# Exponentials shared by three engines: the whole powers made on GpSimd, the gate sums on TensorE, both query masks in one step

## The chip, the cores and the metric

The kernel runs on one core of a Trainium2 chip. The core has five engines with a queue each, which run side by side and wait for each other by semaphores: TensorE (PE; its weight loads are shown as PEld), VectorE (DVE), ScalarE (ACT), GpSimd (POOL) and SyncE (SP), whose queue issues most DMA transfers. Each engine takes its instructions in the order in which they stand. The metric is the device time of one execution in microseconds; lower is better.

## The reference

One input `x` of 2048 rows of 512 goes through an attention block A and a mixer block B; a gate of each row mixes the two.

```python
def _A_ref(x, wqkv, wo):                      # H = 32 heads of Dh = 16
    qkv = (lambda x, *d: x.transpose(*d))((x @ wqkv).reshape(B, S, 3, H, Dh), 2, 0, 3, 1, 4)
    scores = jnp.einsum("bhqd,bhkd->bhqk", q, k) * (Dh ** -0.5)
    p = _softmax(scores, axis=-1)
    o = jnp.einsum("bhqk,bhkd->bhqd", p, v)
    return (lambda x, *d: x.transpose(*d))(o, 0, 2, 1, 3).reshape(B, S, D) @ wo
...
    h = _gelu(_layernorm(x, axis=-1) @ w1)    # B: then four groups of columns shifted by rows, @ w2
    x1 = x + hs
    h2 = _gelu(_layernorm(x1, axis=-1) @ w3) @ w4
    return x1 + h2
...
g = _sigmoid((x * gate_w).sum(-1, keepdims=True))
return g * a + (1 - g) * b
```

All inputs are 16-bit floats (bfloat16). With 32 heads, 2048 queries and 2048 keys there are 134 million exponentials.

## The kernel before, in words

**Attention.** Work goes by units `(c, u)`: a chunk `c` of 512 queries and four heads `u`, 32 units. For each of 16 key tiles `kt` (128 keys) and each head `j` of the unit there is a block of scores, 128 keys by 512 queries, made by one matmul (`score`, L634). Two or three blocks share a stage of PSUM, and one ScalarE instruction takes the exponential of the stage (`expo`, L723) into `pt`; a matmul per block then multiplies `pt` with the values and adds into `acc` (`attend_block`, L731). The 1868 blocks that go this way make 694 exponentials: 34 early ones over two blocks, then two or three blocks each. The code calls each of the 694 a slot.

**The blocks that ScalarE does not do.** In each unit but the first two, 6 of 64 blocks (180 in all) get their exponential from VectorE and GpSimd instead. Their scores go to a PSUM tile `dsc` beside a stage of two blocks. `whole` (L638) then does for one block:

- L652, VectorE: `y`, a 32-bit integer, the score in units of 2^-16 of a power of two. Its upper 16 bits are the whole power, its lower 16 the fraction.
- L657 and L659, GpSimd: from the lower halves (every second 16-bit word of `y`), the two factors `ec` and `ea` of a polynomial, 16-bit floats.

Two blocks make a pair, and when the second is there VectorE does four steps of 1024 elements, each due a slot after the one before, the first three slots after the second block: `square` (L663), `one` (L667), `cubic` (L671, which leaves a bfloat16 between 1 and 2, times a constant) and `power` (L679). `power` takes the upper halves of `y`, times 128, and adds them to the bits of `ec` as 16-bit integers, by a scalar_tensor_tensor; this puts the whole power into the exponent. The pair then goes to TensorE like a `pt` (L731, `acc<-ec,vp`). `y` has two buffers, each of a pair and held from L652 to L679; `ea` has two, `ec` three.

**What sets the order.** The order of each engine's instructions is written out by the kernel: a loop over slots (L884 onward) emits the exponential of slot i, the scores of slot i+2, the matmuls with the values, a portion of other TensorE work (`beside`: projections, the mixer block, output tiles), a filling of idle matmuls with zeros (`fill`, L874), and then the VectorE steps that are due (`run_due`, L558). `due(slots, rank, cost, fn)` puts a step off by some slots. `run_due` sorts what is due by rank, and lets a step wait, by at most four slots, while the kernel's own reckoning of the engines' clocks says that VectorE is too far behind TensorE (`HORIZON`). A step in `asides` is taken one at a slot when there is time. `hurry` forces steps when a third pair or a second chain is open.

Scores of slot k+2 use the banks of slot k. They wait for the exponential of slot k, and where `dsc` was in use, for L652.

**Gate.** For each of 16 row tiles, `gate(t)` (L361) is an aside: VectorE multiplies `x` by the gate weights, spread over all partitions (`gw_b`, L137), and sums them into `g_raw` (L363, with a read of the accumulator). When the last is done, ScalarE takes a tanh (L367), VectorE makes `g_fin` (L369). The asides of the first LayerNorm's statistics (L277) stand between them.

**Query projections.** `q_proj` (L241) makes the queries of two units at once and leaves them in `qT` twice, each time with the other unit's 16 rows of 32 set to zero: two tensor_scalar steps by a mask column (L247).

Of the kernel before, what the change touches and what calls it, by code (L numbers as in the profile page):

```python
# [30 lines left out]
def kernel(  # L31
# [20 lines left out]
    KT = D // P  # L52
    NT = S // P
# [27 lines left out]
    ypool = ctx.enter_context(tc.tile_pool(name="ypool", bufs=2))  # L81
# [12 lines left out]
    gw_b = const.tile([P, D], BF16, name="gw_b")  # L94
# [42 lines left out]
    nc.sync.dma_start(out=gw_b[:], in_=gate_w.partition_broadcast(P))  # L137
# [29 lines left out]
    HORIZON = 1.9  # L167
    OVER = 4
# [72 lines left out]
    def q_proj(c, G):  # L241
        ps = gen("ps_q")
        qT = qpool.tile([P, 2, CH], BF16, tag="qT", name="qT")
        qTs[(c, G)] = qT
        yield from proj(ps, wq, slice(G * P, (G + 1) * P), xT[c])
        for a in range(2):
            evac(0.75).tensor_scalar(out=qT[:, a, :], in0=ps[:], scalar1=mask[:, a:a + 1], scalar2=None,  # L247
                                    op0=ALU.mult)
        made.add(("q", c, G))
        yield MM  # L250
        yield FREE
# [109 lines left out]
    def gate(t):  # L361
        scr = xnpool.tile([P, CH], BF16, tag="xn", name="scr")
        vec(0.77).tensor_tensor_reduce(  # L363
            out=scr[:], in0=x_sb[t][:], in1=gw_b[:], scale=1.0, scalar=0.0,
            op0=ALU.mult, op1=ALU.add, accum_out=g_raw[:, t:t + 1])
        if t == NT - 1:
            due(3, FIRST, 0.0, lambda: nc.scalar.activation(  # L367
                out=g_t[:], in_=g_raw[:], func=ACT.Tanh, scale=0.5))
            due(5, FIRST, 0.2, lambda: nc.vector.tensor_scalar(  # L369
                out=g_fin[:], in0=g_t[:], scalar1=0.5, scalar2=0.5, op0=ALU.mult, op1=ALU.add))  # L370

    def first_asides():
        for t in range(NT):
            asides.append(lambda t=t: ln_stats(0, t))
            asides.append(lambda t=t: gate(t))
        norm(0, 0)
# [109 lines left out]
    def early():  # L486
        for w in "v0 v1 k1 v2 v3 v4 k2 v5 v6 v7 v8 v9 k3 v10 v11 v12 v13 v14 v15".split():
            if w == "v1":
                first_asides()
            yield from (v_proj(int(w[1:])) if w[0] == "v" else k_proj(0, int(w[1:])))  # L490
        for G in range(1, NU // 2):
            for c in range(NC_):
                yield from k_proj(G, c)
            if G == 1:
                yield from q_proj(0, G)
        yield from mlp()
        state["done"] = True
# [60 lines left out]
    def run_due(all=False, only=(FIRST, CHAIN, LAST, TAIL)):  # L558

        now, state["force"] = state["slot"], all  # L560
        for item in sorted((x for x in later if x[0] <= now and x[1] in only), key=lambda x: (x[1], x[0], x[2])):
            _, _, _, cost, fn = item
            if cost and not all and max(clock["vector"], clock["act"]) + cost > clock["pe"] + HORIZON and now < item[0] + OVER:
                continue
            later.remove(item)
            fn()
        if TAIL in only and asides and now >= EARLY // 2 and max(clock["vector"], clock["act"]) + 0.7 < clock["pe"] + HORIZON:
            asides.popleft()()
# [69 lines left out]
    def whole(dsc, c, u, kt, j):  # L638


        if state["half"] == 0:
            while state["pairs"] == 3 or state["chains"] == 2:
                hurry()
            state["pairs"] += 1
            state["chains"] += 1
            halves["now"] = (ypool.tile([P, 2, CH], I32, tag="y", name="y"), epool.tile([P, 2, CH], F16, tag="ea", name="ea"),
                             ecpool.tile([P, 2, CH], F16, tag="ec", name="ec"), [])
        y, ea, ec, pair = halves["now"]
# [3 lines left out]
        vec(0.69, clock["pe"] + 0.2).tensor_scalar(out=y[:, r, :], in0=dsc[:], scalar1=65536.0 * DH ** -0.5 / LN2,  # L652
                                                   scalar2=-126.0 * 65536.0, op0=ALU.mult, op1=ALU.max)
        lo = y[:, r, :].bitcast(U16).rearrange("p (n k) -> p n k", k=2)[:, :, 0]
# [5 lines left out]
                                scalar2=root * CUB * IM * IM * (REAL - LN2 / 2), op0=ALU.mult, op1=ALU.add)  # L660

        def square():
            vec(0.75).tensor_tensor(out=ec[:], in0=ec[:], in1=ec[:], op=ALU.mult)  # L663
            due(1, CHAIN, 0.45, one)

        def one():
            vec(0.45).tensor_scalar(out=ec[:], in0=ec[:], scalar1=1.0, scalar2=None, op0=ALU.add)  # L667
            due(1, CHAIN, 0.7, cubic)

        def cubic():  # L670
            vec(0.75).tensor_tensor(out=ec[:].bitcast(BF16), in0=ec[:], in1=ea[:], op=ALU.mult)  # L671
            due(1, CHAIN, 1.23, power)

        def power():

            bits = ec[:].bitcast(I16)
            hi = y[:].bitcast(I16).rearrange("p r (n k) -> p r n k", k=2)[:, :, :, 1]
            state["chains"] -= 1
            vec(1.23).scalar_tensor_tensor(out=bits, in0=hi, scalar=128.0, in1=bits, op0=ALU.mult, op1=ALU.add)  # L679
            due(1, LAST, 0.0, lambda: products.append((c, u, pair, ec[:].bitcast(BF16))), "pe")  # L680

        if r == 1:
            due(3, CHAIN, 0.7, square)
# [239 lines left out]
```

## Time and profile before

| | |
|---|---|
| Runs shown | 927.56, 933.54, 933.91 us; median 933.54 |
| The profiled execution | 926.85 us, its span 925.1 us |
| Mean granted clock of TensorE | 0.982 |
| ScalarE busy | 884.4 us, 96% of the span |
| VectorE busy | 754.1 us, 82% |
| GpSimd busy | 313.0 us, 34% |
| L723, exponentials | 694, 854.6 us in all |
| L679, power | 90, 117.9 us in all, 1310 ns each |
| L657 and L659, GpSimd's two steps | 180 each, 811 and 828 ns each |
| L363, gate sums | 16, 702 ns each |
| L247, query masks | 30, 744 ns each |

How to read it: busy time is the union of an engine's instructions. A row of a group gives the line, the engine, the operation, output from inputs, shapes and number, then the busy time in us, the mean duration of one in ns, and after a second bar the time that the engine stood idle just before such instructions, with what ended it. Instructions of one engine overlap a little, so that the mean times the number can be more than the busy time: two exponentials over three blocks take 2.79 us together, one of them 1.45. The profile's matmul durations are modelled.

### The profile page before, as it was taken

What the parts mean: (1) busy time and instruction counts of PE and PEld (TensorE: products, weight loads), DVE (VectorE), ACT (ScalarE), POOL (GpSimd) and SP (SyncE); (2) the same over time, 40 slices, a digit from 0 to 9 for tenths busy, and PEclk for the clock granted to TensorE, in tenths of its full rate; (3) what the DMA queues carried; (4) which work ended last, traced back from release to release, by engine and by line L of the source; (5) the groups of instructions that cost most, each with busy time, mean ns of one, the idle gap of its engine ahead of it and who ended that gap; (6) DMA issues with size and microseconds to landing.
All of it is one profiled execution on the core that took longest, in us unless ns stands there. A gap on an engine that the chain in (4) does not pass through costs nothing.

```text
span 925.1 us, 14505 instructions
## 1 busy us (share of the span) xinstructions
PE 796.2 (86%) x5478; PEld 245.1 (26%) x5581; DVE 754.1 (82%) x1160; ACT 884.4 (96%) x735; POOL 313.0 (34%) x401
## 2 busy tenths in 40 slices
PE   7998888888888788899988889988889888889886
PEld 2222322222222222222222222222222222222221
DVE  3778888989899898877899967899976789876656
ACT  6889999999999999999999999999999999999993
POOL 3014334343444333433333333333244234333430
PEclk9998999999999999999999999999999999999998
DMA  9601000000000000000000000100000000000000
GB/s 218 198 13 58 1 13 13 13 14 2 13 12 13 13 13 5 10 13 24 25 13 2 12 13 13 36 13 13 1 12 13 13 13 8 29 13 13 13 13 23
DMA packets 30382, 22.28 MB, mean 24 GB/s; under 512 B 16744, under 2 KB 25832, under 8 KB 30312
## 3 DMA queue, kind: packets, MB, share of 16 engines
q1 hardware_dynamic: 28680, 20.17, 7.6%
q10 hardware_dynamic: 1632, 1.18, 0.5%
q8 instruction: 43, 0.70, 0.3%
q14 instruction: 27, 0.22, 0.1%
HBM read 17.17 MB, written 2.35 MB: 21 GB/s over the span
## 4 chain that ended last, share of the span: by engine, by line
ACT 45%; issue 19%; PE 16%; DVE 15%; DMA 4%; ACTq 0%; DVEq 0%; SPq 0%
ACT pt L723 43%; PE stage L634 5%; PE acc L731 3%; DVE ec L679 2%; DMA bcs<-rec_d 2%; DVE y L652 2%; ACT sq L345 2%; PE ps_k L222 1%; PE ps_v L222 1%; PE acc L874 1%; PE ps_o L222 1%; DMA rec_d<-rec 1%; PE ps L222 1%; DVE ec L671 1%; DVE yh L328 1%
## 5 line engine op out<-in xcount | busy, mean ns | idle before, releaser
L723 ACT ACTIVATE pt<-stage 128x1536 bf16<-128x1536 f32 (+1 forms) x694 | 854.6, 1413 | 20.6 <-PE stage L634 18.1
L634 PE MATMUL stage<-qT,kT 32*128 32x512 bf16 x1868 | 278.3, 387 | 100.9 <-ACT pt L723 73.8
L657 POOL TENSOR_SCALAR ec<-y 128x512 f16<-128x512 uint16 x180 | 145.9, 811 | 504.2 <-DVE y L652 504.0
L731 PE MATMUL acc<-pt,vp 128*17 128x512 bf16 (+1 forms) x1868 | 190.5, 389 | 1.0 <-DVE accsb L766 0.6
L634 PEld LDWEIGHTS <-kT 32*128 32x128 bf16 x2048 | 95.7, 91 | 344.7 <-issue 277.4
L652 DVE TENSOR_SCALAR y<-dsc 128x512 int32<-128x512 f32 x180 | 123.3, 685 | 52.5 <-PE dsc L634 51.0
L659 POOL TENSOR_SCALAR ea<-y 128x512 f16<-128x512 uint16 x180 | 149.1, 828 | 14.3
L874 PE MATMUL acc<-wq,zero 128*128 128x512 bf16 x396 | 137.5, 387 | 4.8 <-issue 4.8
L679 DVE SCALAR_TENSOR_TENSOR ec<-y,ec 128x1024 int16<-128x1024 int16 x90 | 117.9, 1310 | 1.1
L222 PE MATMUL ps_y<-xnT,w 128*128 128x512 bf16 x257 | 88.7, 393 | 3.3 <-DVE yh L328 1.6
L731 PEld LDWEIGHTS <-vp 128*17 128x17 bf16 (+1 forms) x2048 | 49.4, 88 | 121.6 <-issue 117.2
L671 DVE TENSOR_TENSOR ec<-ec,ea 128x1024 bf16<-128x1024 f16 x90 | 67.5, 751 | 3.6
L634 PE MATMUL dsc<-qT,kT 32*128 32x512 bf16 x180 | 70.4, 391 | 0.0
L222 PE MATMUL ps<-w,g2T 128*128 128x512 bf16 x208 | 63.1, 383 | 2.0 <-issue 1.9
L663 DVE TENSOR_TENSOR ec<-ec 128x1024 f16<-128x1024 f16 x90 | 63.2, 703 | 1.5 <-POOL ec L657 1.5
L328 DVE TENSOR_SCALAR yh<-ps_y 128x512 bf16<-128x512 f32 x72 | 49.4, 686 | 18.3 <-PE ps_y L222 16.2
L667 DVE TENSOR_SCALAR ec<-ec 128x1024 f16<-128x1024 f16 x90 | 45.9, 510 | 0.9
L874 PEld LDWEIGHTS <-zero 128*128 128x128 bf16 x430 | 32.9, 98 | 48.8 <-issue 48.6
L345 ACT ACTIVATE sq<-sq 128x1024 bf16<-128x1024 bf16 x36 | 41.6, 1155 | 1.5 <-DVE sq L340 1.5
L349 DVE SCALAR_TENSOR_TENSOR g2T<-sq,yh 128x1024 bf16<-128x1024 bf16 x28 | 38.5, 1379 | 0.0
L731 PE MATMUL acc<-ec,vp 128*17 128x512 bf16 x180 | 35.7, 390 | 2.4 <-DVE ec L679 2.4
L785 DVE TENSOR_TENSOR oT<-accsb,bcs 128x512 bf16<-128x512 f32 x31 | 22.4, 722 | 18.3 <-DMA bcs<-rec_d 18.2
(80 smaller groups left out, 510.7 us busy)
## 6 DMA issues: line engine op xcount, KB each, us to landing
bcs<-rec_d SPq DMA_DIRECT2D x31, 256.0 KB
w<-in_B_w_dram SPq DMA_DIRECT2D x2, 1792.0 KB
x_sb<-in_A_x_dram SPq DMA_DIRECT2D x14, 128.0 KB
out_dram<-ot SPq DMA_DIRECT2D x14, 128.0 KB
w<-in_B_w_dram SPq DMA_DIRECT2D x2, 512.0 KB
wkv<-in_A_wqkv_dram ACTq DMA_DIRECT2D x1, 512.0 KB
wo_pad<-in_A_wo_dram SPq DMA_DIRECT2D x8, 64.0 KB
den<-accsb SPq DMA_DIRECT2D x31, 8.0 KB
```

Of the source, the lines that this page charges most:

```text
L222: nc.tensor.matmul(*args, **kwargs)
L345: nc.scalar.activation(out=sq[:], in_=sq[:], func=ACT.Tanh)
L634: nc.tensor.matmul(out, lhsT=kT[G][32 * j:32 * j + 32, cc, o:o + P], rhs=qTs[(c, G)][32 * j:32 * j + 32, a, :], start=True, stop=True, til ...
L652: vec(0.69, clock["pe"] + 0.2).tensor_scalar(out=y[:, r, :], in0=dsc[:], scalar1=65536.0 * DH ** -0.5 / LN2, scalar2=-126.0 * 65536.0, op0 ...
L657: nc.gpsimd.tensor_scalar(out=ec[:, r, :], in0=lo, scalar1=g / IM, scalar2=(RE - LN2 / 2) / IM, op0=ALU.mult, op1=ALU.add)
L659: nc.gpsimd.tensor_scalar(out=ea[:, r, :], in0=lo, scalar1=root * CUB * IM * IM * g, scalar2=root * CUB * IM * IM * (REAL - LN2 / 2), op0= ...
L663: vec(0.75).tensor_tensor(out=ec[:], in0=ec[:], in1=ec[:], op=ALU.mult)
L671: vec(0.75).tensor_tensor(out=ec[:].bitcast(BF16), in0=ec[:], in1=ea[:], op=ALU.mult)
L679: vec(1.23).scalar_tensor_tensor(out=bits, in0=hi, scalar=128.0, in1=bits, op0=ALU.mult, op1=ALU.add)
L723: nc.scalar.activation(out=pt[:, 0:w], in_=stages.pop(k)[:, 0:w], func=ACT.Exp, scale=DH ** -0.5)
L731: nc.tensor.matmul(accs[(c, u)][32 * j:32 * j + M, :], lhsT=lhsT, rhs=p, start=(kt == 0), stop=(kt == NT - 1), skip_group_check=True, tile ...
L874: nc.tensor.matmul(acc[:], lhsT=zero[:], rhs=wq[:, 0, :], start=False, stop=False, skip_group_check=True)
```

## The change

- `whole` gets a third GpSimd step per block: the upper halves of `y` times 128, as 16-bit floats, into a new tile `nk` (two buffers of a pair). `y` is now a tile of one block, still with two buffers, read by GpSimd alone.
- `power` adds `nk` to the bits of `ec` by a plain tensor_tensor.
- `square` is due two slots after the second block (`CLAG`), not three. The other lags have a name and stay at one.
- The gate's 16 VectorE sums and their asides go. `gates()` runs on TensorE between the last key projection and the mixer block: for each row tile four matmuls of one column, with `x` transposed as the weights, into one PSUM tile; VectorE copies the 16 columns out. The gate weights are loaded as four columns of 128 (`gw`) and not spread over the partitions.
- `q_proj` writes both masked halves by one tensor_tensor, with the projection and the mask broadcast.
- `run_due` picks the next item anew after each step, in place of a list sorted once.

```diff
-    gw_b = const.tile([P, D], BF16, name="gw_b")
+    gw = const.tile([P, KT], BF16, name="gw")
...
-    nc.sync.dma_start(out=gw_b[:], in_=gate_w.partition_broadcast(P))
+    nc.sync.dma_start(out=gw[:], in_=gate_w.rearrange("(kt p) -> p kt", p=P))
...
+    CLAG = 2
+    NLAG = 1
...
-        for a in range(2):
-            evac(0.75).tensor_scalar(out=qT[:, a, :], in0=ps[:], scalar1=mask[:, a:a + 1], scalar2=None,
-                                    op0=ALU.mult)
+        evac(1.25).tensor_tensor(out=qT[:], in0=ps[:].unsqueeze(1).to_broadcast([P, 2, CH]),
+                                 in1=mask[:].unsqueeze(2).to_broadcast([P, 2, CH]), op=ALU.mult)
...
-    def gate(t):
-        scr = xnpool.tile([P, CH], BF16, tag="xn", name="scr")
-        vec(0.77).tensor_tensor_reduce(
-            out=scr[:], in0=x_sb[t][:], in1=gw_b[:], scale=1.0, scalar=0.0,
-            op0=ALU.mult, op1=ALU.add, accum_out=g_raw[:, t:t + 1])
...
+    def gates():
+
+        ps = gen("ps_g")
+        for t in range(NT):
+            c, o = divmod(t * P, CH)
+            clock["pe"] = max(clock["pe"], clock["bank"])
+            for kt in range(KT):
+                nc.tensor.matmul(ps[:, t:t + 1], lhsT=xT[c][:, kt, o:o + P], rhs=gw[:, kt:kt + 1],
+                                 start=(kt == 0), stop=(kt == KT - 1))
+            tensor("full", 0.3)
+            if t < NT - 1:
+                yield 0.3
+        evac(0.2).tensor_copy(out=g_raw[:], in_=ps[:, 0:NT])
+        due(3, FIRST, 0.0, lambda: nc.scalar.activation(out=g_t[:], in_=g_raw[:], func=ACT.Tanh, scale=0.5))
+        due(6, FIRST, 0.2, lambda: nc.vector.tensor_scalar(
+            out=g_fin[:], in0=g_t[:], scalar1=0.5, scalar2=0.5, op0=ALU.mult, op1=ALU.add))
...
-            asides.append(lambda t=t: gate(t))
...
+        yield from gates()
         yield from mlp()
...
-        for item in sorted((x for x in later if x[0] <= now and x[1] in only), key=lambda x: (x[1], x[0], x[2])):
+        passed = []
+        while True:
+            items = [x for x in later if x[0] <= now and x[1] in only and x not in passed]
+            if not items:
+                break
+            item = min(items, key=lambda x: (x[1], x[0], x[2]))
...
+                passed.append(item)
                 continue
...
+        y = ypool.tile([P, CH], I32, tag="y", name="y")
...
+        hi = y[:].bitcast(I16).rearrange("p (n k) -> p n k", k=2)[:, :, 1]
...
+        nc.gpsimd.tensor_scalar(out=nk[:, r, :], in0=hi, scalar1=128.0, scalar2=None, op0=ALU.mult)
...
-            due(1, CHAIN, 1.23, power)
+            due(NLAG, CHAIN, 0.75, power)
...
-            hi = y[:].bitcast(I16).rearrange("p r (n k) -> p r n k", k=2)[:, :, :, 1]
             state["chains"] -= 1
-            vec(1.23).scalar_tensor_tensor(out=bits, in0=hi, scalar=128.0, in1=bits, op0=ALU.mult, op1=ALU.add)
+            vec(0.75).tensor_tensor(out=bits, in0=bits, in1=nk[:], op=ALU.add)
...
-            due(3, CHAIN, 0.7, square)
+            due(CLAG, CHAIN, 0.7, square)
```

More of the change, by code (lines that the diff above doesn't have):

```diff
@@ L52 @@
     KT = D // P
+    YBUFS = 2
     NT = S // P
@@ L80 @@
     fin = ctx.enter_context(tc.tile_pool(name="fin", bufs=1))
-    ypool = ctx.enter_context(tc.tile_pool(name="ypool", bufs=2))
+    ypool = ctx.enter_context(tc.tile_pool(name="ypool", bufs=YBUFS))
+    nkpool = ctx.enter_context(tc.tile_pool(name="nkpool", bufs=2))
     epool = ctx.enter_context(tc.tile_pool(name="epool", bufs=2))
@@ L359 @@
     g_fin = const.tile([P, NT], F32, name="g_fin")
-    def gate(t):
-        scr = xnpool.tile([P, CH], BF16, tag="xn", name="scr")
-        vec(0.77).tensor_tensor_reduce(
-            out=scr[:], in0=x_sb[t][:], in1=gw_b[:], scale=1.0, scalar=0.0,
-            op0=ALU.mult, op1=ALU.add, accum_out=g_raw[:, t:t + 1])
[L366 to L370, printed above, removed]
+    def gates():
[13 more added lines that the diff above has]
+            out=g_fin[:], in0=g_t[:], scalar1=0.5, scalar2=0.5, op0=ALU.mult, op1=ALU.add))
+        yield 0.3
+        yield FREE
     def first_asides():
@@ L645, in whole @@
             state["chains"] += 1
-            halves["now"] = (ypool.tile([P, 2, CH], I32, tag="y", name="y"), epool.tile([P, 2, CH], F16, tag="ea", name="ea"),
+            halves["now"] = (nkpool.tile([P, 2, CH], F16, tag="nk", name="nk"), epool.tile([P, 2, CH], F16, tag="ea", name="ea"),
                              ecpool.tile([P, 2, CH], F16, tag="ec", name="ec"), [])
-        y, ea, ec, pair = halves["now"]
+        nk, ea, ec, pair = halves["now"]
+        y = ypool.tile([P, CH], I32, tag="y", name="y")
         r = state["half"]
@@ L651, in whole @@
         pair.append((kt, j))
-        vec(0.69, clock["pe"] + 0.2).tensor_scalar(out=y[:, r, :], in0=dsc[:], scalar1=65536.0 * DH ** -0.5 / LN2,
+        vec(0.69, clock["pe"] + 0.2).tensor_scalar(out=y[:], in0=dsc[:], scalar1=65536.0 * DH ** -0.5 / LN2,
                                                    scalar2=-126.0 * 65536.0, op0=ALU.mult, op1=ALU.max)
-        lo = y[:, r, :].bitcast(U16).rearrange("p (n k) -> p n k", k=2)[:, :, 0]
+        lo = y[:].bitcast(U16).rearrange("p (n k) -> p n k", k=2)[:, :, 0]
+        hi = y[:].bitcast(I16).rearrange("p (n k) -> p n k", k=2)[:, :, 1]
         g = LN2 / 65536.0
@@ L660, in whole @@
                                 scalar2=root * CUB * IM * IM * (REAL - LN2 / 2), op0=ALU.mult, op1=ALU.add)
+        nc.gpsimd.tensor_scalar(out=nk[:, r, :], in0=hi, scalar1=128.0, scalar2=None, op0=ALU.mult)
         def square():
             vec(0.75).tensor_tensor(out=ec[:], in0=ec[:], in1=ec[:], op=ALU.mult)
-            due(1, CHAIN, 0.45, one)
+            due(NLAG, CHAIN, 0.45, one)
         def one():
             vec(0.45).tensor_scalar(out=ec[:], in0=ec[:], scalar1=1.0, scalar2=None, op0=ALU.add)
-            due(1, CHAIN, 0.7, cubic)
+            due(NLAG, CHAIN, 0.7, cubic)
         def cubic():
             vec(0.75).tensor_tensor(out=ec[:].bitcast(BF16), in0=ec[:], in1=ea[:], op=ALU.mult)
-            due(1, CHAIN, 1.23, power)
+            due(NLAG, CHAIN, 0.75, power)
         def power():
             bits = ec[:].bitcast(I16)
-            hi = y[:].bitcast(I16).rearrange("p r (n k) -> p r n k", k=2)[:, :, :, 1]
             state["chains"] -= 1
-            vec(1.23).scalar_tensor_tensor(out=bits, in0=hi, scalar=128.0, in1=bits, op0=ALU.mult, op1=ALU.add)
+            vec(0.75).tensor_tensor(out=bits, in0=bits, in1=nk[:], op=ALU.add)
             due(1, LAST, 0.0, lambda: products.append((c, u, pair, ec[:].bitcast(BF16))), "pe")
         if r == 1:
-            due(3, CHAIN, 0.7, square)
+            due(CLAG, CHAIN, 0.7, square)
     def scores(k):
```

## The prediction

> **What bounds the kernel now.** I read the page first: the busy shares, then the costliest groups (busy us, mean ns of one, then the engine's idle time before them and what ended it).
>
> ```profile
> PE 796.2 (86%) x5478; PEld 245.1 (26%) x5581; DVE 754.1 (82%) x1160; ACT 884.4 (96%) x735; POOL 313.0 (34%) x401
> ...
> L723 ACT ACTIVATE pt<-stage 128x1536 bf16<-128x1536 f32 (+1 forms) x694 | 854.6, 1413 | 20.6 <-PE stage L634 18.1
> ...
> L657 POOL TENSOR_SCALAR ec<-y 128x512 f16<-128x512 uint16 x180 | 145.9, 811 | 504.2 <-DVE y L652 504.0
> ...
> L679 DVE SCALAR_TENSOR_TENSOR ec<-y,ec 128x1024 int16<-128x1024 int16 x90 | 117.9, 1310 | 1.1
> ...
> L671 DVE TENSOR_TENSOR ec<-ec,ea 128x1024 bf16<-128x1024 f16 x90 | 67.5, 751 | 3.6
> ...
> L663 DVE TENSOR_TENSOR ec<-ec 128x1024 f16<-128x1024 f16 x90 | 63.2, 703 | 1.5 <-POOL ec L657 1.5
> ```
>
> ScalarE's 694 exponentials (one per 854.6/694 = 1.23 us) fill the span; the change keeps all 694 and the 36 tanh, as the order of the built program shows. So only ScalarE's idle 925.1 − 884.4 = 40.7 us can move. The busy time by stretch says where that is:
>
> ```profile
> 0.00:60.00 60.00, 52.78 (x304) 16.20 (x310) 34.20 (x75) 43.80 (x44) 10.47 (x33) 0.97 0.63 162
> 60.00:100.00 40.00, 36.65 (x254) 10.97 (x255) 33.22 (x66) 37.87 (x32) 13.72 (x18) 0.91 0.13 38
> 100.00:900.00 800.00, 690.77 (x4838) 213.32 (x4927) 671.39 (x1001) 791.77 (x654) 288.77 (x351) 0.99 0.04 13
> 900.00:925.10 25.10, 15.96 (x92) 4.61 (x92) 15.30 (x20) 10.93 (x8) 0.00 (x0) 0.87 0.06 21
> ```
>
> (The fourth busy figure is ScalarE's.) It idles 16.2 us before 60 (loads, then TensorE's projections), 2.1 in 60 to 100, only 8.2 in 100 to 900, 14.2 at the end. The timeline names each gap of the 8.2; this is one of them:
>
> ```profile
> 801.92 1.22 DVE L679 SCALAR_TENSOR_TENSOR ec<-y,ec 128x1024 int16<-128x1024 int16 x1
> ...
> 803.66 0.69 DVE L652 TENSOR_SCALAR y<-dsc 128x512 int32<-128x512 f32 x1
> ...
> 804.41 0.39 PE L634 MATMUL stage<-qT,kT 32*128 32x512 bf16 x3 [1.11 <-DVE y L652]
> ...
> 804.90 1.45 ACT L723 ACTIVATE pt<-stage 128x1536 bf16<-128x1536 f32 x1 [0.85 <-PE stage L634]
> ```
>
> The power step (and the next pair's square, at 803.06) stand ahead of y on VectorE; the next scores wait 1.11 for y, which frees their bank; the exponential comes 0.85 late. Sorted by such causes: VectorE late (y, the power step, the GELU's sq), nine gaps, 0.32+0.16+0.59+0.56+0.24+0.54+0.93+0.20+0.85 = 4.4 us; TensorE at half the granted clock (stretches of 3.4 us from 151, 331, 465, 663, 741), 2.7; runs of five or more projections between two scores, 1.1. The waits put it in proportion:
>
> ```profile
> PEld L634 <- DVE y L652: 30.8, 51, 1.6
> ...
> PE stage L634 <- DVE y L652: 7.9, 15, 1.1
> ```
>
> TensorE's loads and matmuls wait 38.7 us for y in all, yet ScalarE's gaps of that kind are a ninth of it: the scores are made about one exponential ahead, so that lead has to be used up first. VectorE at 82% is thus not the bound, and an engine made lighter is worth here only what it takes out of the few late cases.
>
> **The change, part by part.**
>
> *Power step.* 90 × 1.310 leave VectorE. The two-operand add of 1024 16-bit elements has a near row on either side: 0.703 (L663, one tensor twice) and 0.751 (L671, two tensors); if it is not packed, 1.31 stays. I take L671's: 67.6 against 117.9, −50.3 us.
>
> *Whole powers on GpSimd.* 180 × 0.811 (L657; fastest 0.617, longest 1.862) = +146 us, 313 to 459, half the span. Its queue gets a third instruction per block. From the end of ea to the next ec's start it has 2.77 us in the median, 0.51 at the least, 1.22 at the twentieth, so nk fits nearly always. The add comes 3.6 us or more after ea's end by today's spacing, so it finds nk made: hidden, by less than a slot more if GpSimd is held up. A buffer of nk is written again two pairs later, some 18 us on, when its add is long past; y, now one block a buffer and read by GpSimd alone, is written again two blocks later, 9 us on. What stays uncovered is the square, moved from three slots behind y to two: today it starts 2.82 us after the second ec ends (median), 1.64 at the tenth, 1.07 at the twentieth, 0.03 at the least. Less 1.23, about one square in fifteen would wait, with y and the evacuations behind it on VectorE's queue and the scores behind y. I charge ScalarE +0.3 us; bounds 0 and 13 (rival D).
>
> *Contention.* VectorE's steps run longer where GpSimd runs beside more than 60% of them: L663 0.660 alone, 0.714 beside; L671 0.684 and 0.783; the tensor_scalar L667 0.416 and 0.615. The excess over undisturbed ones is some 31 us in all VectorE groups; with 459/313 of the GpSimd time, +14.
> The Trainium skill ("SBUF — State Buffer", section "Who interferes with whom") speaks against this change: such VectorE steps and a GpSimd step that reads SBUF exclude each other, and the second "fully blocks". By it each nk would cost its whole 0.617, +111 in place of +14. The trace agrees that they slow each other, but the lengthening seen (0.05 to 0.20 us) is far less than 0.617; starts put off are not ruled out.
>
> *Gate sums.* Sixteen VectorE sums leave, 11.2 + 1.3 = −12.5 us, one copy comes (+0.2). In their place come 64 one-column matmuls with 128x128 loads, in some eight slots after the key projections. Nearest row: four 128-column transposes with such loads take 0.40 us, 0.06 each after the first; above, 0.097, the load's own row. So 4 to 6 us of TensorE, up to 16 in one slot (1.0 to 1.6 us against 1.23 of lead): +0.4 us for ScalarE, bounds 0 and 1.2. The gate-weight load stays on SP's queue ahead of the wo, w3 and w4 loads, in smaller pieces; before's issue took 0.50 us at 20 us, and the gate matmuls come 60 us later: 0.
>
> *Masks.* A pair took 1.41 us in the timeline; one step of 1024 at full width is nearest to L679's 1.22 undisturbed (0.75 if packed, 1.4 disturbed): 15 × −0.2 = −2.9.
>
> VectorE: 754 − 50 − 12 − 3 + 14 = about 703. What ScalarE gets of it: in three gaps (0.59, 0.93, 0.85) a power step stands directly ahead and ends 0.56 sooner, −1.7; of the other 2.0 of that kind I take half, −1.0 (bounds together 0 and −4.4). What is late next there is GELU's last step, L349, 1.38 us long in places ahead of y, which the change leaves. In 60 to 100, 1.7 us of gaps follow a wait of 1.12 for y at 83 and a half-clock stretch from 82.3 to 89.1; half, −0.8 (bounds 0, −1.7). At 48.8 a 2.9 us wait for kT stays: LN statistics take the gates' place in the queue. The end: before, two fillers and two late ec products run between the last pt products and the copy of acc (912.5 to 913.4); in the new order they stand earlier, −0.65. The tail behind it is the same. The new loop in run_due picks the same items, since every follow-up is due a slot later at the earliest: 0.
>
> Sum: −1.7 − 1.0 − 0.8 − 0.65 + 0.4 + 0.3 = −3.45: 926.85 to 923.4. The profiled execution is 0.7% under the median, 933.54; the four executions shown (926.85, 927.56, 933.54, 933.91) lie in two groups, mean 930.5, for a cause that no view shows. I put the forecast beside that mean, +3.6: **927.0**.
>
> **Rivals.**
> - B, more: all late gaps, the half-clock ones and those at 82 to 90 go: 4.4 + 2.7 + 1.7 + 0.65 = 9.4, 917.5, with the +3.6: 921. For: some stretches of half clock follow starved matmuls. Against: others follow none that VectorE caused.
> - C, nothing: the add is not packed or the gaps just move; 930.5. For: ScalarE felt a tenth of VectorE's lateness.
> - E, the two engines shut each other out: each of 180 nk holds a VectorE step for the 0.617 of L657's shortest; VectorE 754 − 65 + 111 = 800, busier than before, and lateness of 4.4 + 1.7 half as long again, +3: 933.5. Against: the measured lengthening. This is the Trainium skill's rule, cited under contention.
> - D, slower: the square, now first in VectorE's queue a slot earlier, waits for GpSimd's ec. If it holds the queue 1.0 us on average, the y's behind pass the exponential's lead: today y starts more than 0.90 us after its scores in a quarter of cases; 180 / 4 × 0.3 = +13: 943.5. It decides from a mean wait of about 0.9 us. Against: 1.6 us of median slack left.
>
> **How the numbers follow.** A, the forecast: 0.56, own range 921 to 933. B 0.12, C 0.15, E 0.07, D 0.10. The range 919.5 to 936.5 leaves out D and the lower half of B. Over 1% (about what a measurement of this kernel can tell from no change) faster means under 924.2: B and a quarter of A, 0.26. Slower means over 942.9: D, 0.10. Within: 0.64.
>
> **What would show it.** The add's row at 0.70 to 0.80 with 90 of them; nk near 0.8; POOL about 459, DVE about 703; ACT idle in 100 to 900 down from 8.2 to about 5.5; a small wait of the square for ec. A square waiting often, or ScalarE's gaps unchanged at VectorE 703, would make it wrong.

## The result, and the profile after

The changed kernel takes 939.88 us (median of 20 runs) against 930.56 us for the kernel before on the same chip (20 runs): ratio 1.0089, 95% interval 1.0069 to 1.011. It is slower by 0.9%, where 927.0 us and a small gain were forecast. A run that stands far above the others of its kernel (here one of 1106.13 us, at a granted clock of 0.556) is left out of every ratio. The profiled execution took 940.16 us, its span 938.4, at a mean granted clock of 0.963 (before: 0.982). The two profiled executions lie 13.3 us apart and the medians 9.3, because the one of before (926.85 us) was among its quicker ones.

The page of the changed kernel: the busy shares, then the groups that answer to those shown of before (busy us, mean ns of one, then the engine's idle time before them and its causes).

```profile
PE 830.3 (88%) x5650; PEld 248.3 (26%) x5650; DVE 726.4 (77%) x1114; ACT 887.6 (95%) x735; POOL 606.3 (65%) x581
...
L742 ACT ACTIVATE pt<-stage 128x1536 bf16<-128x1536 f32 (+1 forms) x694 | 853.5, 1377 | 29.8 <-PE stage L651 24.3
...
L680 POOL TENSOR_SCALAR nk<-y 128x512 f16<-128x512 int16 x180 | 306.1, 1701 | 14.3
L676 POOL TENSOR_SCALAR ec<-y 128x512 f16<-128x512 uint16 x180 | 132.2, 735 | 235.5 <-DVE y L670 232.6
...
L698 DVE TENSOR_TENSOR ec<-ec,nk 128x1024 int16<-128x1024 int16 x90 | 77.4, 860 | 5.6
...
L683 DVE TENSOR_TENSOR ec<-ec 128x1024 f16<-128x1024 f16 x90 | 72.1, 801 | 8.3 <-POOL ec L676 7.7
L691 DVE TENSOR_TENSOR ec<-ec,ea 128x1024 bf16<-128x1024 f16 x90 | 72.2, 802 | 3.8
```

VectorE did get lighter, by 28 us (754.1 to 726.4). But nk takes 1701 ns, twice its price, the square and L691 each grew (703 to 801, 751 to 802), and the exponentials now wait 24.3 us for TensorE where they waited 18.1. (The trace of before has 5478 matmul records beside 5581 weight loads, the trace here 5650 of both. Some records of before are thus missing, so TensorE's busy times are not compared.)

Busy time by stretch, changed kernel; the fourth busy figure is ScalarE's, and the one behind GpSimd's is the granted clock.

```profile
0.00:60.00 60.00, 54.33 (x303) 16.53 (x303) 34.11 (x73) 42.78 (x43) 12.20 (x35) 0.94 0.62 160
60.00:100.00 40.00, 38.34 (x340) 13.07 (x337) 23.04 (x41) 39.84 (x34) 20.46 (x23) 1.00 0.15 39
100.00:900.00 800.00, 709.69 (x4845) 210.56 (x4843) 647.26 (x972) 779.84 (x641) 563.67 (x515) 0.97 0.04 13
900.00:938.40 38.40, 27.90 (x178) 8.10 (x176) 22.00 (x31) 25.13 (x20) 9.95 (x10) 0.91 0.06 21
```

ScalarE's idle time by these rows, against before: 17.2 (16.2), 0.2 (2.1), **20.2 (8.2)**, 13.3 (14.2). The span grew 13.3 us: 12.0 of it is idle time in 100 to 900 and 3.2 is more busy time, while the other stretches idle 1.8 us less. So the loss is spread through the middle of the kernel. The waits of the changed kernel over its whole span (us in total, times, longest):

```profile
DVE oT L804 <- DMA bcs<-rec_d: 24.7, 20, 3.1
...
PEld L651 <- DVE y L670: 23.8, 39, 1.9
...
DVE ec L683 <- POOL ec L676: 7.7, 10, 1.4
PE stage L651 <- DVE y L670: 5.8, 7, 1.6
```

TensorE waits less for y than before (29.6 against 38.7), the square waits for GpSimd (before: 1.5 us in 3 waits), and one wait has grown that the prediction did not name: VectorE's `oT`, which multiplies a finished attention tile by reciprocals that come back by DMA, from 18.2 us in 13 waits to 24.7 in 20. Its row before was:

```profile
DVE oT L785 <- DMA bcs<-rec_d: 18.2, 13, 2.7
```

The timeline shows one of these (start, duration, instruction, idle time before it and its cause):

```profile
265.14 2.39 ACT L742 ACTIVATE pt<-stage 128x1024 bf16<-128x1024 f32 x2
...
265.94 0.69 DVE L804 TENSOR_TENSOR oT<-accsb,bcs 128x512 bf16<-128x512 f32 x1 [1.72 <-DMA bcs<-rec_d]
...
266.55 0.69 DVE L280 BATCH_NORM_STATS2 st<-x_sb 128x6 f32<-128x512 bf16 x1
267.27 0.18 DVE L281 BATCH_NORM_AGGREGATE mv<-st 128x2 f32<-128x6 f32 x1
267.37 0.66 DVE L670 TENSOR_SCALAR y<-dsc 128x512 int32<-128x512 f32 x1
...
268.08 0.39 PE L651 MATMUL stage<-qT,kT 32*128 32x512 bf16 x3 [1.39 <-DVE y L670]
...
268.58 1.45 ACT L742 ACTIVATE pt<-stage 128x1536 bf16<-128x1536 f32 x1 [1.05 <-PE stage L651]
```

Read it downwards: VectorE stands 1.72 us at `oT`, with statistics and y behind it in its queue; y frees the bank 1.39 us late for TensorE's scores; the exponential is 1.05 us late.

### The profile page after: what moved, and what is told of

Same layout as the page of the kernel before. It is cut to its first block, busy times and chain, and to the rows that moved or that the text cites. A ratio compares the mean times of both kernels' runs of the same rounds, so it can differ in the third digit from the quotient of the medians.

```text
span 938.4 us, 14922 instructions
## 1 busy us (share of the span) xinstructions
PE 830.3 (88%) x5650; PEld 248.3 (26%) x5650; DVE 726.4 (77%) x1114; ACT 887.6 (95%) x735; POOL 606.3 (65%) x581
## 4 chain that ended last, share of the span: by engine, by line
ACT 39%; PE 23%; issue 18%; DVE 14%; DMA 7%; DVEq 0%; ACTq 0%; SPq 0%
ACT pt L742 38%; PE stage L651 7%; DMA bcs<-rec_d 5%; PE acc L750 5%; PE acc L893 2%; PE ps L226 2%; PE ps_y L226 2%; DVE y L670 1%; PE ps_k L226 1%; DMA rec_d<-rec 1%; DVE st L280 1%; DVE ec L683 1%; PE ps_v L226 1%; DVE oT L804 1%; DVE ec L691 1%
## 5 line engine op out<-in xcount | busy, mean ns | idle before, releaser
L742 ACT ACTIVATE pt<-stage 128x1536 bf16<-128x1536 f32 (+1 forms) x694 | 853.5, 1377 | 29.8 <-PE stage L651 24.3
L651 PE MATMUL stage<-qT,kT 32*128 32x512 bf16 x1868 | 282.3, 393 | 89.0 <-ACT pt L742 65.1
L680 POOL TENSOR_SCALAR nk<-y 128x512 f16<-128x512 int16 x180 | 306.1, 1701 | 14.3
L676 POOL TENSOR_SCALAR ec<-y 128x512 f16<-128x512 uint16 x180 | 132.2, 735 | 235.5 <-DVE y L670 232.6
L750 PE MATMUL acc<-pt,vp 128*17 128x512 bf16 (+1 forms) x1868 | 193.9, 396 | 0.6 <-DVE accsb L785 0.6
L893 PE MATMUL acc<-wq,zero 128*128 128x512 bf16 x435 | 152.0, 395 | 0.0
L226 PE MATMUL ps_y<-xnT,w 128*128 128x512 bf16 x288 | 99.4, 395 | 4.9 <-DVE yh L331 4.2
L698 DVE TENSOR_TENSOR ec<-ec,nk 128x1024 int16<-128x1024 int16 x90 | 77.4, 860 | 5.6
L683 DVE TENSOR_TENSOR ec<-ec 128x1024 f16<-128x1024 f16 x90 | 72.1, 801 | 8.3 <-POOL ec L676 7.7
L691 DVE TENSOR_TENSOR ec<-ec,ea 128x1024 bf16<-128x1024 f16 x90 | 72.2, 802 | 3.8
L226 PE MATMUL ps<-w,g2T 128*128 128x512 bf16 x224 | 66.8, 385 | 0.2 <-DVE x_sb L412 0.2
L331 DVE TENSOR_SCALAR yh<-ps_y 128x512 bf16<-128x512 f32 x72 | 49.2, 684 | 13.3 <-PE ps_y L226 12.7
L804 DVE TENSOR_TENSOR oT<-accsb,bcs 128x512 bf16<-128x512 f32 x31 | 25.0, 808 | 24.8 <-DMA bcs<-rec_d 24.7
```

What stands on the lines that cost most here:

```text
L226: nc.tensor.matmul(*args, **kwargs)
L651: nc.tensor.matmul(out, lhsT=kT[G][32 * j:32 * j + 32, cc, o:o + P], rhs=qTs[(c, G)][32 * j:32 * j + 32, a, :], start=True, stop=True, til ...
L676: nc.gpsimd.tensor_scalar(out=ec[:, r, :], in0=lo, scalar1=g / IM, scalar2=(RE - LN2 / 2) / IM, op0=ALU.mult, op1=ALU.add)
L680: nc.gpsimd.tensor_scalar(out=nk[:, r, :], in0=hi, scalar1=128.0, scalar2=None, op0=ALU.mult)
L698: vec(0.75).tensor_tensor(out=bits, in0=bits, in1=nk[:], op=ALU.add)
L742: nc.scalar.activation(out=pt[:, 0:w], in_=stages.pop(k)[:, 0:w], func=ACT.Exp, scale=DH ** -0.5)
```

## The experiments

All times are ratios to the kernel before on the same chip, with 95% intervals. Where an edit says "the part alone", the other parts of the change are left off the kernel before. The planner is the kernel's own reckoning of engine time: the number in `vec(...)` and `due(...)` says what it believes a VectorE step costs, and so what it lets stand where. The letters of the theories in the expectations are their own and not those of the prediction's rivals.

### The parts one by one

**The changed kernel with nk in a two-operation form.**

```diff
-nc.gpsimd.tensor_scalar(out=nk[:, r, :], in0=hi, scalar1=128.0, scalar2=None, op0=ALU.mult)
+nc.gpsimd.tensor_scalar(out=nk[:, r, :], in0=hi, scalar1=128.0, scalar2=0.0, op0=ALU.mult, op1=ALU.add)
```

> The changed kernel with one thing altered: GpSimd's third step has two operations (times 128, plus 0.0) like its two neighbours, not one. Theory T1 (the whole powers are slow as written: 1.49 us at the least against 0.62 for the two-operation steps, and GpSimd at 606 us disturbs VectorE and delays ec): the step falls to 0.62 at the least and some 0.85 in the mean, POOL to about 455 us, the square's wait for ec from 7.7 to about 2 us, and the time from 939.9 to between 926 and 932. Theory T2 (the order of the queues, not GpSimd's load, costs the time: gates on TensorE, the lags, VectorE lighter): whatever the step does, the time stays at 937 to 942. If the step stays at 1.49, the slow part is the signed 16-bit input and not the missing second operation.

1.0062 (1.0033 to 1.0091), 936.21 us. GpSimd's group:

```profile
L680 POOL TENSOR_SCALAR nk<-y 128x512 f16<-128x512 int16 x180 | 147.1, 817 | 14.2
```

The same product from the same 16-bit integers, with an addition of zero added, takes 817 ns in place of 1701 (the shortest 620 in place of 1488). So the one-operation form was the slow thing, and the forecast's 811 was the price of the other form. But with 159 us taken off GpSimd the kernel is only about 0.3% faster, and the intervals overlap: the time fell into neither theory's range, and the slow step is the smaller part of the loss.

**The power part alone** (nk in one operation, the plain add; the square still three slots on).

```diff
+nc.gpsimd.tensor_scalar(out=nk[:, r, :], in0=hi, scalar1=128.0, scalar2=None, op0=ALU.mult)
...
-            due(1, CHAIN, 1.23, power)
+            due(1, CHAIN, 0.75, power)
...
-vec(1.23).scalar_tensor_tensor(out=bits, in0=hi, scalar=128.0, in1=bits, op0=ALU.mult, op1=ALU.add)
+vec(0.75).tensor_tensor(out=bits, in0=bits, in1=nk[:], op=ALU.add)
```

> The kernel before with the power part alone: GpSimd's third step (one operation, as in the change), y of one block, the two-operand add; the square is still due three slots after the second block, gates and masks as before. T1: most of the loss is here, 935 to 940 against 930.6, POOL at about 600 us. T2: nothing here, 928 to 932, and a TensorE mean clock near before's 0.98.

1.0153 (1.011 to 1.0197), 944.6 us: slower than the whole change, and more than either theory gave. Here `y`, now one block a buffer, also waits for the slow step to have read it, which the prediction ruled out: 8.8 us in 4 waits, the longest 3.0. In the changed kernel the waits show none of these.

**The gates part alone** (`gates()` in place of the 16 asides, as in the change).

```diff
-            asides.append(lambda t=t: gate(t))
...
+        yield from gates()
         yield from mlp()
```

> The kernel before with the gate sums on TensorE alone. T1: within 0.3% of before, 928 to 933, VectorE 12 us less busy. T2: the gates hold the one PSUM bank and shift the mixer block, 934 to 938.

1.0156 (1.0104 to 1.0208), 947.19 us, also slower than the whole change, and beyond both theories. Taken exponential by exponential, the delay against before comes in steps: +2.7 us at the exponentials 60 to 80, where the sums stand, but also +6.2 at 140 to 180, +5.1 at 380 to 400 and +6.3 at 440 to 460, hundreds of us after the last gate matmul. The timeline at the last of these, gates part alone:

```profile
605.03 0.55 SPq L789 DMA_DIRECT2D bcs<-rec_d  x1
...
609.75 0.69 DVE L793 TENSOR_TENSOR oT<-accsb,bcs 128x512 bf16<-128x512 f32 x1 [4.36 <-DMA bcs<-rec_d]
610.36 0.42 DVE L338 TENSOR_SCALAR sq<-sq 128x1024 bf16<-128x1024 bf16 x1
610.81 0.69 DVE L340 TENSOR_TENSOR sq<-sq,yh 128x1024 bf16<-128x1024 bf16 x1
611.42 0.68 DVE L660 TENSOR_SCALAR y<-dsc 128x512 int32<-128x512 f32 x1
611.54 1.06 ACT L345 ACTIVATE sq<-sq 128x1024 bf16<-128x1024 bf16 x1 [3.56 <-DVE sq L340]
...
612.16 0.61 PE L642 MATMUL stage<-qT,kT 32*128 32x512 bf16 x3 [3.79 <-DVE y L660]
```

The fetch of the reciprocals is issued at 605.03; VectorE has nothing left ahead of `oT` at 605.39 and stands 4.36 us. Behind it are the GELU's sq, whose tanh holds ScalarE's queue for 3.56 us, and y, for which TensorE stands 3.79. Another `oT` waits 3.27 us at 523.8, just ahead of ScalarE's wait of 1.87 for sq at 529.2.

**The masks part alone.**

```diff
-        for a in range(2):
-            evac(0.75).tensor_scalar(out=qT[:, a, :], in0=ps[:], scalar1=mask[:, a:a + 1], scalar2=None,
-                                    op0=ALU.mult)
+        evac(1.25).tensor_tensor(out=qT[:], in0=ps[:].unsqueeze(1).to_broadcast([P, 2, CH]),
+                                 in1=mask[:].unsqueeze(2).to_broadcast([P, 2, CH]), op=ALU.mult)
```

> The kernel before with the query masks in one step alone, 15 steps of 1.22 us for 30 of 0.74. T1: 929 to 932, no difference to be measured. T2: at most a part of the loss, since queries arrive together: up to 934.

0.9988 (0.9961 to 1.0015), 929.98 us: no difference. Two parts thus cost 1.5% each alone and 0.9% together. Costs that belonged to the instructions themselves would add.

### Is it the wait for the reciprocals?

The edit is the same in all three: `oT` is due later behind the reciprocal, so that its DMA has landed.

```diff
-            due(5, FIRST, 0.7, scale)
+            due(8, FIRST, 0.7, scale)
```

In the changed kernel with the two-operation nk:

> The changed kernel with the GpSimd step that makes the whole powers in its two-operation form, and the step that multiplies a finished attention tile by the fetched reciprocals (oT) put 8 slots behind the reciprocal instead of 5. Theory A (a lighter VectorE reaches that step before its DMA has landed; everything queued behind it, y above all, comes late, TensorE starves and falls to half clock): the waits of oT for the DMA fall from 24.5 us to under 8 us, half-clock stretches from 14 to at most 10, time about 930 us, ratio to the kernel before 0.997 to 1.002 against 1.006 with the step at 5 slots. Theory B (that wait stands where VectorE has slack anyway; the lost time is made elsewhere): the waits for the DMA fall as said, but the time stays near 936 us, ratio 1.005 or more.

1.0047 (1.002 to 1.0074), against 1.0062 at five slots. The waits of `oT` for the DMA went from 24.5 us to none, the half-clock stretches of the whole span from 14 to 10, and the time hardly moved.

In the kernel before:

> The kernel before with that one step at 8 slots instead of 5. Theory A: oT waits for the DMA fall from 18.2 us to under 5 us and the time by 2 to 5 us, 926 to 928 us, ratio 0.994 to 0.998. Theory B: ratio 0.998 to 1.004, no gain.

0.9956 (0.9937 to 0.9975), 925.43 us. A gain, and a version that beats both kernels. Here `oT`'s 18.2 us of waits fell to 0.1.

In the gates part alone:

> The kernel before with the gates part alone (1.0156 to the kernel before) and the oT step at 8 slots instead of 5. In the profile of the gates part alone the oT step stood 4.36 us at 605.4 us waiting for its DMA, y behind it came late, TensorE stood 3.79 us and ScalarE 3.56 us. Theory A: that stall and its like go, ScalarE's waits for VectorE's sq fall from 5.6 to under 2 us, ratio 1.002 to 1.007, 933 to 937 us. Theory B: other stalls take its place, ratio 1.011 or more, 941 us or more.

1.0006 (0.9974 to 1.0037), against 1.0156. ScalarE's waits for sq, 5.6 us, no longer stand among its waits. The ratio is even below theory A's range. So theory A holds for the gates part: nearly its whole loss went with this one number, while the 64 matmuls stayed. It does not hold for the whole change, where the late step gave 0.15%. Moving the step also moves what stands behind it, so the edit is not the wait alone.

**The gate sums left out.**

```diff
+    def gate():
+        nc.gpsimd.memset(g_raw[:], 0.1)
...
-            asides.append(lambda t=t: gate(t))
+            if t == NT - 1:
+                asides.append(gate)
```

> The kernel before with the gate sums left out: the 16 gate values are set to a constant, so neither VectorE nor TensorE makes the sums; 16 VectorE steps of 0.78 us are gone and nothing comes in their place. Theory D (taking VectorE work away moves the order for the worse): ratio 1.008 to 1.016, as slow as with the sums on TensorE, 940 to 946 us. Theory E (the 64 one-column matmuls and the PSUM bank that they hold, at 60 to 100 us, are what made the gates part cost 1.6%): ratio 0.994 to 1.001, 925 to 931 us.

1.000 (0.9971 to 1.0029). Theory D is wrong for the gates: taking the sums off VectorE did no harm. It also did no good, though 12.5 us of VectorE were gone. The order moved in this run too, so another order does not always cost. Theory E's reason, the matmuls and their bank, does not stand either, since with `oT` at eight slots the same matmuls cost nothing. The harm came where both met: the sums on TensorE, and `oT` at five slots.

### The order or the durations?

**The power part alone, two-operation nk.**

> The kernel before with the power part alone (GpSimd makes the whole powers, VectorE adds them; the square still 3 slots behind), but with the GpSimd step in its two-operation form. Theory C (the slow one-operation step, 1.70 us where 0.82 was counted on, is what made the power part alone cost 1.5%): ratio 0.998 to 1.004, about 931 us. Theory D (the lighter VectorE moves the order of its steps for the worse, whatever GpSimd takes): ratio 1.008 or more, about 939 us, with POOL about 447 us busy all the same.

1.0121 (1.0094 to 1.0147), 940.16 us. Theory C falls: with GpSimd at 445 us in place of 600 the part still costs 1.2%.

**The same, with the planner told the old cost.** The instructions are those of the last kernel; the order is that of the kernel before on TensorE, ScalarE, VectorE and SyncE, and the two traces bear this out (735 steps on ScalarE, 1160 on VectorE, 5581 weight loads on TensorE, in the same sequence).

```diff
-            due(1, CHAIN, 0.75, power)
+            due(1, CHAIN, 1.23, power)
...
-            vec(0.75).tensor_tensor(out=bits, in0=bits, in1=nk[:], op=ALU.add)
+            vec(1.23).tensor_tensor(out=bits, in0=bits, in1=nk[:], op=ALU.add)
```

> The kernel before with the power part alone, in its two-operation form (1.0121 to the kernel before), but with the planner still told the old cost of the VectorE step, 1.23 where it now takes 0.75: the order of the instructions is then that of the kernel before on TensorE, ScalarE, VectorE and SyncE, and only the durations differ (VectorE about 50 us lighter, GpSimd about 145 us heavier). Theory D (the cheaper cost lets the planner put steps earlier, and that order costs the 1.2%): ratio 0.994 to 1.003, 925 to 933 us. Theory F (the durations cost it: GpSimd holds y and lengthens VectorE's steps beside it): ratio 1.008 or more, about 940 us.

**0.9953** (0.9922 to 0.9984), 927.26 us, faster than both kernels. The middle stretch, with the old cost told:

```profile
100.00:900.00 800.00, 696.11 (x4850) 214.15 (x4940) 650.34 (x1001) 792.88 (x655) 414.81 (x523) 0.99 0.04 13
```

and with the new cost told, with the same steps on ScalarE, VectorE and GpSimd:

```profile
100.00:900.00 800.00, 692.62 (x4780) 210.52 (x4867) 644.04 (x988) 781.79 (x644) 410.91 (x517) 0.98 0.04 13
```

ScalarE idles 7.1 us there with the old cost and 18.2 with the new one. Exponential by exponential, the old-cost kernel gains some 4 us by exponential 240 and ends 3.5 us ahead of the profiled execution of before; the new-cost kernel falls behind from exponential 240 on and ends 12.3 us late.

**The new order under the old durations.** The kernel before, every instruction kept; only the planner is told 0.75 for a step that takes 1.31.

```diff
-            due(1, CHAIN, 1.23, power)
+            due(1, CHAIN, 0.75, power)
...
-            vec(1.23).scalar_tensor_tensor(out=bits, in0=hi, scalar=128.0, in1=bits, op0=ALU.mult, op1=ALU.add)
+            vec(0.75).scalar_tensor_tensor(out=bits, in0=hi, scalar=128.0, in1=bits, op0=ALU.mult, op1=ALU.add)
```

> The kernel before with every instruction kept, and only the planner told 0.75 for its power step, which still takes 1.31: the order of TensorE, ScalarE, VectorE and SyncE is then that of the power part alone in its two-operation form (1.0121). Theory D: the order by itself costs, ratio 1.010 to 1.025, 941 to 955 us. Theory H (the order loses only together with GpSimd's added work): ratio 1.005 or less.

1.0134 (1.010 to 1.0169), 943.87 us. Its middle stretch:

```profile
100.00:900.00 800.00, 710.81 (x4844) 209.74 (x4842) 663.15 (x986) 777.88 (x640) 286.10 (x344) 0.97 0.04 13
```

ScalarE idles 22.1 us, though no step of ScalarE, VectorE or GpSimd was added, dropped or shortened. What the planner writes costs 1.3% by itself, more than the whole change. That is the order and one thing more: the planner also sets how many idle matmuls with zeros go between, and here it puts in 21 more than before (and the same 451 in the power part alone). The weight loads of these fillers, in the kernel before and then here:

```profile
L874 PEld LDWEIGHTS <-zero 128*128 128x128 bf16 x430 | 32.9, 98 | 48.8 <-issue 48.6
```

```profile
L874 PEld LDWEIGHTS <-zero 128*128 128x128 bf16 x451 | 34.4, 98 | 53.6 <-issue 53.4
```

Their number does not go with the loss over all runs: the gates part with the late `oT` has 463 at a ratio of 1.0006, the changed kernel 435 at 1.0089. But no run held the order and changed the filling, so below "the order" means both.

**Told 1.0**, between the two (the same two numbers, 1.0 in place of 0.75).

> The power part alone in its two-operation form, with the planner told 1.0 for the VectorE step: between 0.75 (ratio 1.0121) and 1.23 (ratio 0.9953). Theory D, steady form (the lower the told cost, the earlier the steps, the more is lost): ratio 1.001 to 1.007. Theory D, chance form (each told cost makes some other order, and orders scatter): as likely below 0.998 or above 1.009 as between.

1.0009 (0.9984 to 1.0034). 1.23, 1.0, 0.75 give 0.9953, 1.0009, 1.0121: between, at the lower edge of the steady form. The chance form gave that even odds, and three points of one step do not make a rule.

**GpSimd's added work alone.** The kernel before, in which GpSimd also makes the whole powers into a tile that its next step overwrites; the order of the others is kept.

```diff
+        hi_r = y[:, r, :].bitcast(I16).rearrange("p (n k) -> p n k", k=2)[:, :, 1]
+        nc.gpsimd.tensor_scalar(out=ea[:, r, :], in0=hi_r, scalar1=128.0, scalar2=0.0, op0=ALU.mult, op1=ALU.add)
```

> The kernel before with GpSimd making the whole powers in the two-operation form beside its own work, into a tile that its next step overwrites, so that nobody uses them: VectorE keeps its long step, and the order of all engines' other instructions stays. It adds GpSimd's 146 us alone. Theory F: VectorE's steps beside GpSimd lengthen, ec and ea come later, ratio 1.004 to 1.015. Theory D: ratio 0.998 to 1.003, since the order has not moved and GpSimd has room.

1.013 (1.008 to 1.0179), 943.04 us. The busy shares, and TensorE's wait for y in 100 to 900 (before: 28.5 us in 48 waits):

```profile
PE 807.8 (86%) x5478; PEld 244.3 (26%) x5581; DVE 780.6 (83%) x1160; ACT 887.5 (94%) x735; POOL 473.8 (50%) x581
```

```profile
PEld L634 <- DVE y L652: 44.7, 60, 2.2
```

161 us of GpSimd that nobody uses lengthen VectorE's steps by 26.5 us (754.1 to 780.6) and cost 1.3%. So contention, the lengthening of one engine's steps beside the other's, is real too: theory F, where the prediction had 14 us of it. With the shorter add, VectorE is 23 us lighter than before all the same (730.9), and then the sum is a gain.

### The whole change

**The changed kernel, told the old cost** (the same two numbers, in the changed kernel).

> The changed kernel as it is, its one-operation GpSimd step kept; only the planner is told 1.23 for the power step, as before the change, instead of 0.75. Theory D (the cheaper cost makes an order that loses): ratio to the kernel before 0.999 to 1.004, against 1.0089 for the changed kernel. Theory G (in the whole change the gate sums and the masks have moved the order already, so the told cost of one step decides nothing): ratio 1.007 or more.

1.0071 (1.0043 to 1.010), against 1.0089: theory G. The told cost of one step does not put the order back; that the gate sums and masks have moved it already is the likely reason, but no run shows it.

**The square at three slots again.**

```diff
-    CLAG = 2
+    CLAG = 3
```

> The changed kernel with one number put back: the square stands 3 slots behind its pair again, not 2. If the square's waits for GpSimd are a cost of the whole change (7.7 us in 10 waits, against 1.5 us in 3 before): those waits fall to about 2 us and the ratio from 1.0089 to 1.001 to 1.006. If VectorE has room where they stand: the waits fall as said and the ratio stays at 1.007 to 1.011.

1.007 (1.0043 to 1.0097). The square's waits for GpSimd, 7.7 us in 10, became:

```profile
DVE y L670 <- POOL nk L680: 5.4, 3, 3.0
...
DVE ec L683 <- POOL ec L676: 0.5, 1, 0.5
```

The first row is new here: `y` now waits 5.4 us in 3 waits for GpSimd to have read its buffer. So the run takes one wait away and brings another. The difference to the changed kernel, 0.2%, is within the intervals.

**All four mendings in the changed kernel:** nk in two operations, the old cost told, `oT` at eight slots, the square at three.

> The whole change with the four mendings that the runs so far gave or that one of this pair tests: GpSimd's step in the two-operation form, the old cost told for the power step, the oT step 8 slots behind the reciprocal, the square 3 slots behind its pair. If the mendings add (1.0089 less 0.0027 for the form, 0.0018 for the told cost, 0.0015 for the late step, and what the square gives): ratio 1.000 to 1.003, about 932 us. If each just makes another order: anywhere from 0.994 to 1.009.

1.002 (0.9988 to 1.0051): level with the kernel before, and clear of the changed kernel's 1.0089. Four edits, none of which alone moved the whole by more than 0.3%, take away most of the loss together. The result is what their sum gives, but the other theory's range holds it too, so the run does not choose between them.

**Two that gained nothing together.** The late `oT` with the masks part, on the kernel before:

> The two parts that gain, alone: both query masks in one step (0.9988 to the kernel before) and the oT step at 8 slots (0.9956). If they add: ratio 0.993 to 0.997, 924 to 927 us. If the order that each makes is what counts, and not its sum: anywhere from 0.993 to 1.003.

1.0006 (0.998 to 1.0031), where 0.9988 times 0.9956 would be 0.994. And with the power part at the old cost:

> The power part alone in its two-operation form, the planner told the old 1.23, and the oT step 8 slots behind the reciprocal: the order is that of the kernel before with the late oT step (0.9956), only the durations differ. If a lighter VectorE gains wherever the order stays: 0.9956 times 0.9953, ratio 0.989 to 0.993, about 923 us, below both kernels. Rival (the late oT step has already taken what the lighter VectorE gained): ratio 0.994 to 0.998.

0.9964 (0.9941 to 0.9987), where 0.991 was to come if the gains added. They do not.

## Why the prediction was wrong, point by point

- **The step that failed is the one that gives ScalarE its gain** ("What ScalarE gets of it: in three gaps ... −1.7 ... −1.0 ... −0.8"). Each term was read off a gap of the old order as if the order stayed. It does not: the code works the order out from the told costs, and these changed. For the end the prediction did read the new program's order; here it did not. Under the power part's new order the same instructions cost +1.2%, and that order costs +1.3% with the old instructions; with the gate sums' new order the loss lies in stalls at `oT`. In the changed kernel ScalarE's idle time in 100 to 900 rose from 8.2 to 20.2 us, where it was to fall to 5.5.
- **Where the order was held, the sign was right, and the size by luck.** The power part took −3.5 us in the trace, ratio 0.9953, as the three terms have it. But GpSimd's added work alone costs 1.3%, for which the sum has almost nothing, so the shorter add must have given back some 1.8%. That is an estimate from two medians of one chip (943.04 and 927.26 us, 15.8 apart); the two kernels also differ in where the third step stands and in `y`'s buffers. Two terms, each several times as large as forecast, nearly cancel.
- **Gate sums, +0.4 us, bounds 0 and 1.2:** the part alone cost 1.56%, some 14.5 us. The matmuls were priced; what the new order does further on was not. With `oT` later the part costs 0.06%, so the price was that of a stall far from the edit. The prediction named the waits for y and the square, but never listed VectorE's wait for bcs, 18.2 us in the trace that it had.
- **nk, 180 × 0.811:** 1.701. The row it came from does two operations, and two are faster than one here. GpSimd 606 us, not 459. Worth about 0.3%, at the edge of what the runs tell.
- **Contention, +14 us:** 26.5 us by GpSimd's added work alone. VectorE came to 726, not 703: the add 77.4 where 67.6 was forecast, the square 72.1 (before 63.2), L691 72.2 (67.5). Rival E, the two engines shutting each other out, gave VectorE 111 us more for 180 such steps, and 800 in all; the 180 steps alone lengthened it by 26.5. Its time, 933.5, was nearer than the forecast. The two engines do hinder each other, at 1.3% where nothing else changed; with the order held and the shorter add it was outweighed, so E alone does not make the loss.
- **The add at L671's price, near 0.75:** right. 684 to 693 ns in the three with no GpSimd step beside them, 860 in the mean.
- **y "is written again two blocks later, 9 us on":** put at nothing in the sum. In the changed kernel no wait shows, but with the one-operation `nk` and the square at three slots `y` waits for its buffer, 8.8 us (power part alone) and 5.4 us (whole change).
- **The square's nearer slot, +0.3 us, and rival D:** the square does wait, 7.7 us in all, 0.09 us on average over 90. That is far from the 0.9 from which D was to decide. With the square at three slots the kernel is 0.2% faster, within the intervals. D's time of 943.5 came near the result for a reason that was not the cause.
- **Masks, −2.9 us:** the 15 steps took 18.3 us with the part alone, the 30 before 21.1, ratio 0.9988. **The end, −0.65:** from the last exponential to the end of the span it took 12.16 us against 12.97, −0.8. Both right.
- **"A square waiting often, or ScalarE's gaps unchanged at VectorE 703, would make it wrong":** ScalarE's gaps more than doubled in the middle at VectorE 726, so here the sign of an engine's load did not give the sign of the result.

**What stays open.** For the whole change no run holds the old order with all the new instructions; that its loss, too, is the order's is argued from the parts. The power part's order costs 1.3%; what in it does was not settled, nor what its 21 added fillers do. `oT`'s wait is one way that is shown (the gates part), and the whole change without that wait (and with the two-operation `nk`) still loses 0.5%. The power part's order was not run under the old durations with `oT` late. The half-clock stretches below go with the loss, but no run made or removed them by themselves.

## What to carry to other kernels

Where a kernel's own cost numbers write the instruction order, a changed cost is two changes: run the new instructions in the old order (tell the planner the old cost) and the old instructions in the new order, before you believe either a gain or a loss. When the bound engine lives on a lead of one step, look for waits on a DMA round trip in the queue that feeds it, and try giving those steps slack: here that gained 0.4% in the kernel before and 1.5% in the gates part, though next to nothing in the whole change. Take a price only from a row with the same form, operation count included.

## What the runs showed of the hardware

**One operation slower than two.** On GpSimd a tensor_scalar of 128x512 from 16-bit integers to 16-bit floats took at least 1488 ns with one operation and 617 to 620 with two. The Trainium skill ("GPSIMD Engine Reference", section "3.1 Elementwise — side-by-side cycle accounting") has one price per element for k up to 2, which I read as operations on an element; an estimate from it would be 512 × 1.03 cycles at its 1.2 GHz, 0.44 us, for either form. The trace does not agree: neither row is that low, and the two differ by 0.87 us.

**Half clock after windows that were not idle.** (The granted clock is the share of TensorE's full clock that the profile shows.) Between 60 and 900 us the granted clock fell to half in 6 stretches before and 11 after, each of 3.4 us or a multiple, all at one phase of a 3.413 us raster. Three windows of that raster in the changed kernel:

```profile
251.98:255.39 3.41, 1.91 (x17) 0.68 (x16) 3.38 (x7) 3.41 (x4) 3.13 (x4) 1.00 0.00 0
255.39:258.80 3.41, 3.41 (x15) 0.76 (x13) 1.65 (x4) 1.81 (x2) 1.63 (x1) 0.50 0.02 2
258.80:262.20 3.40, 3.40 (x25) 0.87 (x23) 2.93 (x7) 3.37 (x3) 1.29 (x2) 1.00 0.04 5
```

TensorE worked 1.91 of 3.41 us in the first, and of the matmuls that started there one used the full 128x128 array; the clock halves in the second, and ScalarE, which was full in the first, works 1.81 us. Ahead of the eleven stretches of the changed kernel TensorE was busy for 36 to 64% of the window. Ten of the eleven followed a window with 1 to 4 full-array matmuls, where 5 is the median of the other windows; but 61 of the 245 others have as few, so this does not make a rule. The Trainium skill ("TensorE: Matmul & The Clock Gate", section "What's actually happening") gives this window, 3413 ns, free-running, and the two rates; the trace agrees on both. Its table puts the half rate after at least one idle window, and here TensorE was busy for 56% of the one ahead, by the profile's modelled durations.

Over the profiled executions of all 20 kernels, the time at half clock between 60 and 900 us ran from 17 us (span 922.1) to 65 us (span 945.5), with a correlation of 0.85 to the span; `oT`'s wait for its DMA has 0.50. Whether the half clock lengthens the span or a starved TensorE makes both was not separated. In one execution (the square at three slots) the clock stood at 0.949 in place of 1.00 outside its half-clock stretches, and its span, 933.7 us, was no longer for it than its median led to expect.
